# Nine unread products of 16 columns behind the unread product that follows the turning of Q(0)

## The chip, the cores and the metric

The kernel runs on one core of one Trainium2 chip. The metric is the device time in microseconds (us) of one execution. The engines are named as in the profile: PE is the matrix engine TensorE (PEld are its weight loads), DVE is VectorE, ACT is ScalarE, POOL is GpSimd and SP is SyncE, which here only issues DMA transfers. Line numbers (L633) are those of the kernel before the change.

## The reference

What is computed is a recurrence over 768 tokens for 4 x 8 heads of 48 columns, and then a gated feed-forward block over its output, rearranged to 3072 tokens of 384 columns. All of it is in fp32.

```python
# q, k, v: (4, 8, 768, 48), beta: (4, 8, 768)
k_n = k / (np.linalg.norm(k, axis=-1, keepdims=True) + 1e-06)
state = np.zeros((B, H, D, D))
for t in range(S):
    kt, vt, bt = k_n[:, :, t], v[:, :, t], beta[:, :, t, None]
    y[:, :, t] = einsum('bhd,bhde->bhe', q[:, :, t], state)
    v_old = einsum('bhde,bhd->bhe', state, kt)
    state = state + bt[:, :, :, None] * einsum('bhd,bhe->bhde', kt, vt - v_old)
x = y.transpose(0, 2, 1, 3).reshape(3072, 384)
g = x @ w_gate                                   # w_gate, w_val: (384, 1536)
out = (g * (1 / (1 + exp(-g))) * (x @ w_val)) @ w_out    # w_out: (1536, 384)
```

## The kernel before

The 768 tokens are cut into 12 chunks of 64. For each chunk `c` the recurrence is solved in closed form from small products: K times its transpose and Q times the transpose of K (64 x 64 for each head), the inverse of a triangular matrix, and products with the running state. The feed-forward block takes the tokens of a chunk as soon as its output x is there. Its weights are loaded and converted in pieces while the first chunks are prepared.

The whole order of instructions on PE, ACT, DVE, SP and POOL is written by hand: each engine executes its instructions in the order in which the program issues them, under a manual schedule, and semaphores between the engines are the only waits. There is no planner that would move an instruction.

The first part of the program prepares the chunks 0 to 3. The names that matter:

- `turned(c, of_q)` (L484 to L488) transposes K or Q of chunk c on PE, eight transposes of 128 x 128 into two PSUM banks, and ACT copies the two banks to SBUF (`kt`, `qt`). For K(0), K(1) and Q(0) it copies each bank as it is ready (L486), later both at the end (L488).
- `first_gram(c)` (L640) and `gram_steps(c, of_q)` (L498) are the 64x64x64 products of 32 heads, four of which share the PE array at a time. Their results are copied by ACT (L518, L523).
- `low_copies(c)` (L667) are ACT's copies of parts of the first products.
- `first_substitution()` (L700, L706) and `first_z()` (L710) are the triangular inverse on DVE, and `spread_z` (L723, L725) its spreading into `zt`.
- `n_products(c)` (L733) are the next products of 32 heads on PE, which read `zt`; `n_copies` (L739) takes them out.
- `first_advance()` (L952 and following lines), `advance(c)` (L1138 to L1236) and `of_state(c)` (L921) are the steps of the recurrence; `gate_val` (L1562) and the later forms (L1405, L1682) the feed-forward products.
- `stage(n)` (L261, L262) issues on SP the load of one piece of a weight.
- `unread(count, p, m=512)` (L633) issues `count` products on PE whose result nobody reads. Each multiplies a constant 128 x 32 tile `half` with one column of it, repeated m times, and writes 32 rows and m columns of a PSUM bank that is free at that moment:

```python
    def unread(count, p, m=512):
        for _ in range(count):
            nc.tensor.matmul(p[0:R, 0:m], half, half[:, 0:1].to_broadcast([128, m]))
```

The program before the change has unread products in six places: three ahead of the first transposes, one behind the turning of Q(0), four ahead of n_products, and two single ones of 256 columns between the transposes of the first output. The order around the change is this:

```python
        for n in range(6):
            stage(n, n - 2 if n > 1 else None)
        unread(1, banks("p_t", "py")[0])
        turned(2, False, "py")
        first_q = [gram_steps(0, True, 0, (copy_a, copy_a))]
        next(first_q[0])
        gram(2, False, "px", (copy_a, copy_a))
```

The unread product and the transposes of K(2) behind it write the same pair of PSUM banks, `p_py`.

Of the kernel before, what the change touches and what calls it, by code (L numbers as in the profile page):

```python
# [20 lines left out]
def kernel(  # L21
# [51 lines left out]
    def ps_pair(name, tag):  # L73

        return pairs_of_banks[tag]
# [7 lines left out]
    def ps_ffn(shape, name, bank=None):  # L83
        if bank is None:
            taken.append(name)
            bank = (len(taken) - 1) % 4
        n = 1
        for m in shape[1:]:
            n *= m
        p = ffn_banks[bank][:, 0:n]  # L90
        return p if len(shape) == 2 else p.rearrange("p (x n) -> p x n", x=shape[1])
# [16 lines left out]
    def kn_of(c):  # L108
        return knp[c if c < AHEAD else c % 2]

    def kt_of(c):
        return kts[c] if c < AHEAD else kts_late[c % 4]
# [47 lines left out]
    def load_blocks(of_q, c, pars=(0, 1)):  # L160

        x, _, t = blocks_of[of_q]
        x_v = x.rearrange("b (j par) s d -> par s b j d", par=2)
        t_v = t.rearrange("p bp h d -> p (bp h d)")
        t_v = t_v.rearrange("p (b j blk d) -> p b j blk d", b=B, j=NJ, blk=C // R)
        for par in pars:
            for at in range(0, D, R):
                m = min(R, D - at)
                rows = slice(64 * par + at, 64 * par + at + R)
                for blk in range(C // R):  # L170
                    lo = c * C + R * blk
                    nc.sync.dma_start(
                        out=t_v[rows, :, :, blk, 0:m].rearrange("p b j d -> p (b j) d"),
                        in_=x_v[par, lo : lo + R, :, :, at : at + m].rearrange(
                            "s b j d -> s (b j) d"
                        ),
                    )
# [75 lines left out]
    def stage(n, after=None, queue=nc.sync):  # L253
        _, src, t, f0, m = pieces[n]
        name, lo = place_of[n]
        if name not in places:
            places[name] = words(p_places[0])
        place = places[name][:, lo : lo + 2 * m]
        staged[n] = place
        if after is not None:  # L260
            nc.gpsimd.tensor_copy(place[:, 0:1], staged[after][:, 0:1])  # L261
        queue.dma_start(  # L262
            out=place, in_=src[t * 128 : (t + 1) * 128, f0 : f0 + m].bitcast(U32)
        )
# [187 lines left out]
    def banks(name, tag):  # L452

        if type(tag) is int:
            return [ps_ffn([128, 512], name, tag + i) for i in range(2)]
        p = ps_pair(name, tag)
        return [p[:, 0], p[:, 1]]

    def turned(c, of_q, tag=None):

        if tag is None:
            tag = "py" if of_q else "px"
        x = qpad[c % QB] if of_q else kn_of(c)
        if of_q:
            xt = work.tile([128, NB * NJ * 2 * C], FP32, name="qt", bufs=1)
        else:
            xt = kt_of(c)
        if c >= blocks_of[of_q][1]:
            xt_v = xt.rearrange("p (b bp j i) -> p bp j b i", bp=NB, b=2, j=NJ)
            (qt if of_q else kt)[c] = xt_v  # L470
            blocks = blocks_of[of_q][2]
            nc.vector.transpose(xt, blocks.rearrange("p bp h d -> p (bp h d)"))
            spent.append(1.8)
            if c + 1 < NCH:
                for par in range(2):
                    late_loads.append(lambda par=par: load_blocks(of_q, c + 1, (par,)))
            return
        xt = xt.rearrange("p (bp j b i) -> p bp j b i", bp=NB, j=NJ, b=2)
        (qt if of_q else kt)[c] = xt
        p_t = banks("p_t", tag)  # L480
        for bp in range(NB):
            for j in range(NJ):
                at = slice(128 * j, 128 * j + 128)
                nc.tensor.transpose(p_t[bp][:, at], x[:, bp, 2 * j : 2 * j + 2], ident)  # L484
            if type(tag) is int:
                nc.scalar.copy(xt[:, bp].rearrange("p j b i -> p (j b i)"), p_t[bp])  # L486
        for bp in range(NB if type(tag) is not int else 0):
            nc.scalar.copy(xt[:, bp].rearrange("p j b i -> p (j b i)"), p_t[bp])  # L488
# [141 lines left out]
# [4 lines that stand above are left out]
# [1285 lines left out]
    with tc.manual_schedule(  # L1919
# [34 lines left out]
        for n in range(6):  # L1954
            stage(n, n - 2 if n > 1 else None)
        unread(1, banks("p_t", "py")[0])
        turned(2, False, "py")
        first_q = [gram_steps(0, True, 0, (copy_a, copy_a))]
        next(first_q[0])
# [147 lines left out]
```

## Time and profile before

| | |
|---|---|
| median of three runs | 663.82 us (661.48 to 665.75) |
| the profiled execution | 663.32 us |
| span of its instructions | 661.6 us |
| mean granted TensorE clock | 0.995 |
| PE busy | 649.8 us (98%), 10854 records |
| PE weight loads busy | 596.5 us (90%) |
| DVE, ACT, POOL busy | 475.0, 281.3, 198.7 us |
| instruction queue q8 | 85 packets, 1.39 MB |

The span runs from the first to the last instruction of the program; the rest of the execution's time lies around it. A busy share is an average over the span; PE is at 98% because of the long feed-forward part, while its idle time lies mostly in the first 70 us. A product in fp32 appears as two records of PE, each with a weight load (PEld) of its own. "issue" as the reason of an idle time means that the engine waited for nothing that the profile shows.

### The profile page before, as it was taken

What the parts mean: (1) busy time and instruction counts of PE and PEld (TensorE: products, weight loads), DVE (VectorE), ACT (ScalarE), POOL (GpSimd) and SP (SyncE); (2) the same over time, 40 slices, a digit from 0 to 9 for tenths busy, and PEclk for the clock granted to TensorE, in tenths of its full rate; (3) what the DMA queues carried; (4) which work ended last, traced back from release to release, by engine and by line L of the source; (5) the groups of instructions that cost most, each with busy time, mean ns of one, the idle gap of its engine ahead of it and who ended that gap; (6) DMA issues with size and microseconds to landing.
All of it is one profiled execution on the core that took longest, in us unless ns stands there. A gap on an engine that the chain in (4) does not pass through costs nothing.

```text
span 661.6 us, 24916 instructions
## 1 busy us (share of the span) xinstructions
PE 649.8 (98%) x10854; PEld 596.5 (90%) x10854; DVE 475.0 (72%) x989; ACT 281.3 (43%) x626; POOL 198.7 (30%) x312
## 2 busy tenths in 40 slices
PE   8989999999999999999999999999999999999997
PEld 4667888767999999999999999999999999999997
DVE  6779699999689767758667758667758655655563
ACT  4887757224435433434532533532433432333230
POOL 8030041013894032880031881030882000000000
PEclk8989999999999999999999999999999999999999
DMA  9659763005742451364464264364263442232220
GB/s 138 144 165 265 214 145 119 1 14 92 201 78 73 97 122 51 84 142 89 99 127 92 61 152 104 81 131 105 62 142 88 93 109 67 58 97 65 81 72 25
DMA packets 147438, 68.57 MB, mean 104 GB/s; under 512 B 123456, under 2 KB 126560, under 8 KB 147328
## 3 DMA queue, kind: packets, MB, share of 16 engines
q1 hardware_dynamic: 144832, 66.28, 42.8%
q8 instruction: 85, 1.39, 0.9%
q10 hardware_dynamic: 2240, 0.59, 0.5%
q0 software_dynamic: 256, 0.10, 0.2%
q14 instruction: 25, 0.20, 0.1%
HBM read 59.08 MB, written 7.86 MB: 101 GB/s over the span
## 4 chain that ended last, share of the span: by engine, by line
PE 86%; DVE 7%; SPq 3%; issue 2%; DMA 1%; ACT 1%; POOL 0%; DVEq 0%; ACTq 0%; POOLq 0%
PE ffn L1405 39%; PE ffn L1682 21%; PE ffn L1562 9%; PE ffn L1591 2%; SPq L139 2%; PE p_px L1167 2%; PE p_py L498 1%; DVE x_t L583 1%; DVE zb L589 1%; PE p_px L921 1%; PE p_py L1069 1%; PE p_py L1086 1%; PE p_px L1150 1%; PE p_px L498 1%; SPq L185 1%
## 5 line engine op out<-in xcount | busy, mean ns | idle before, releaser
L1405 PE MATMUL ffn<-x_t,w_gv 128*128 128x128 f32 x800 | 108.7, 279 | 0.9 <-DVE p_sb L1632 0.8
L1405 PEld LDWEIGHTS ffn<-x_t,w_gv 128*128 128x128 f32 x800 | 97.4, 192 | 4.1 <-DVE p_sb L1632 2.0
L1439 ACT ACTIVATE sil<-ffn 128x256 f32<-128x256 f32 x100 | 36.4, 383 | 115.3 <-PE ffn L1405 108.0
L1405 PE MATMUL ffn<-x_ffn,w_gv 128*128 128x128 f32 x640 | 84.6, 275 | 0.0
L1682 PE MATMUL ffn<-wo_sb,h_f 128*128 128x192 f32 x480 | 83.9, 328 | 0.0
L1682 PEld LDWEIGHTS ffn<-wo_sb,h_f 128*128 128x128 f32 x480 | 77.9, 190 | 0.6
L1405 PEld LDWEIGHTS ffn<-x_ffn,w_gv 128*128 128x128 f32 x640 | 78.0, 192 | 0.3
L820 POOL TENSOR_TENSOR n_b<-mb,half 128x32 f32<-128x32 f32 x5 | 27.9, 5582 | 161.4 <-DVE mb L552 161.4
L583 POOL TENSOR_TENSOR h_f<-zb,mb 128x31 f32<-128x31 f32 (+15 forms) x124 | 69.4, 559 | 19.2 <-PE p_py L798 6.0
L589 POOL TENSOR_TENSOR zb<-zb,h_f 128x31 f32<-128x31 f32 (+15 forms) x124 | 70.8, 571 | 9.7
L1405 PE MATMUL ffn<-x_t,h_f 128*128 128x128 f32 x472 | 64.7, 280 | 0.0
L1405 PEld LDWEIGHTS ffn<-x_t,h_f 128*128 128x128 f32 x472 | 57.3, 192 | 1.6 <-DVE ffn L1632 0.5
L1440 DVE TENSOR_TENSOR h_f<-sil,ffn 128x256 f32<-128x256 f32 x100 | 39.3, 418 | 24.0 <-ACT sil L1439 24.0
L1101 ACT COPY x_ffn<-p_py 32x256 f32<-32x256 f32 (+3 forms) x108 | 39.4, 365 | 29.0 <-PE p_py L1086 27.3
L1632 DVE TENSOR_TENSOR ffn<-p_sb,ffn 128x512 f32<-128x512 f32 x40 | 27.8, 696 | 25.9 <-PE ffn L1405 25.2
L1635 DVE TENSOR_TENSOR ffn<-ffn,p_sb 128x512 f32<-128x512 f32 x40 | 27.5, 691 | 19.9 <-PE ffn L1405 19.0
L1682 PE MATMUL ffn<-last_k,h_f 128*128 128x192 f32 x200 | 36.0, 327 | 0.0
L1635 DVE TENSOR_TENSOR o_sb<-o_sb,ffn 128x192 f32<-128x192 f32 x50 | 17.5, 350 | 24.2 <-PE ffn L1682 23.5
L1562 PE MATMUL ffn<-x_t,w_gv 128*128 128x256 f32 x144 | 33.9, 385 | 0.2 <-DVE x_t L1041 0.2
L1682 PEld LDWEIGHTS ffn<-last_k,h_f 128*128 128x128 f32 x200 | 32.9, 190 | 0.1
L1562 PE MATMUL ffn<-x_ffn,w_gv 128*128 128x256 f32 x144 | 31.9, 380 | 0.0
L1405 PE MATMUL ffn<-x_ffn,h_f 128*128 128x128 f32 x232 | 30.9, 276 | 0.0
(330 smaller groups left out, 1171.8 us busy)
## 6 DMA issues: line engine op xcount, KB each, us to landing
h_f<-w_s SPq DMA_DIRECT2D x81, 256.0 KB, 2.8
more_w<-w_s SPq DMA_DIRECT2D x27, 256.0 KB, 2.7
vin<-in_v_dram SPq DMA_DIRECT2D x48, 96.0 KB, 3.5
out_dram<-o_sb SPq DMA_DIRECT2D x46, 96.0 KB, 2.2
kn<-in_k_dram SPq DMA_DIRECT2D x20, 192.0 KB, 4.5
zt<-in_moe_w_out_dram SPq DMA_DIRECT2D x10, 384.0 KB, 4.2
qpad<-in_q_dram SPq DMA_DIRECT2D x36, 64.0 KB, 3.0
w_s<-h_f SPq DMA_DIRECT2D x7, 256.0 KB, 2.6
```

The costliest lines, as they stand in the source:

```text
L139: dmas[b % len(dmas)].dma_start(out=t[64 * b : 64 * b + 64, :, :, 0:D].rearrange("p bp h d -> p (bp h) d"), in_=halves(x, c, b).rearrange( ...
L583: engine.tensor_tensor(out=t_v, in0=zb[:, 0 : j + 1, j : j + 1].to_broadcast([128, j + 1, m]), in1=mb[:, j : j + 1, j + 1 : R].to_broadcas ...
L589: engine.tensor_tensor(out=zb[:, 0 : j + 1, j + 1 : R], in0=zb[:, 0 : j + 1, j + 1 : R], in1=t_v, op=ALU.add,)
L820: nc.gpsimd.tensor_tensor(out=n, in0=mb.rearrange("p j i -> p (j i)")[:, 0 : R * R : R + 1], in1=half, op=ALU.pow,)
L1101: nc.scalar.copy(x_all[at % 128 : at % 128 + rows, at // 128].rearrange("p (bp b i) -> p bp b i", bp=NB, b=2), p[64 * half + lo : 64 * hal ...
L1405: nc.tensor.matmul(p[:, u], w(u), moving, start=start and u == 0, stop=True, skip_group_check=True,)
L1439: nc.scalar.activation(silu_of, p[:, 0:2], ACTF.Silu)
L1440: nc.vector.tensor_tensor(out=h_of(c, PAIRS[r][e % 3], e // 3), in0=silu_of, in1=p[:, 2:4], op=ALU.mult)
L1562: nc.tensor.matmul(ps[name][:, i], w_sb[:, t, (f + i) * 128 : (f + i + 1) * 128], xts[c][:, t], start=(t == 0 and i == 0), stop=(t == KT - 1),
L1632: nc.vector.tensor_tensor(out=out, in0=a, in1=b, op=ALU.subtract)
L1635: nc.vector.tensor_tensor(out=out, in0=a, in1=b, op=ALU.add)
L1682: nc.tensor.matmul(p[x, part], a(f - f % 2)[:, f % 2], b(f), start=not begun and f == 0, stop=f == FH - 1, skip_group_check=True,)
```

## The change

Behind the single unread product that follows the turning of Q(0), and ahead of the transposes of K(2), nine more unread products are issued. Each has 16 columns in the place of 512, and writes to the same bank.

```diff
         for n in range(6):
             stage(n, n - 2 if n > 1 else None)
         unread(1, banks("p_t", "py")[0])
+        unread(9, banks("p_t", "py")[0], 16)
         turned(2, False, "py")
         first_q = [gram_steps(0, True, 0, (copy_a, copy_a))]
```

The instructions of ACT, DVE, POOL and SP stay the same and in the same order; on PE, nine products stand between the unread product and the first transpose of K(2), and everything else is as it was.

## The prediction

> **What bounds the kernel now.** I read the page's busy line and slices first, then the waits of PE (TensorE matmul), then PE's timeline around the edit, then stretches cut by the clock.
>
> ```profile
> span 661.6 us, 24916 instructions
> PE 649.8 (98%) x10854; PEld 596.5 (90%) x10854; DVE 475.0 (72%) x989; ACT 281.3 (43%) x626; POOL 198.7 (30%) x312
> ...
> q8 instruction: 85, 1.39, 0.9%
> ```
>
> PE is busy 649.8 of 661.6 us. All that it idles is 11.8 us, so hardly anything can be gained, and whatever delays PE at a place without a wait behind it goes into the end. The edit sits 16.7 us into the span, in the preparation, where PE and ACT hand work to each other:
>
> ```profile
> 15.11 1.67 PE L633 MATMUL p_py<-half 128*32 128x512 f32 x2
> 16.71 1.09 PE L484 MATMUL p_py<-ident,kn 128*128 128x128 f32 x8
> 17.74 1.16 PE L498 MATMUL ffn<-qt,kt 64*64 64x64 f32 x64
> 19.44 1.18 PE L498 MATMUL p_px<-kt 64*64 64x64 f32 x64 [0.55 <-ACT kt L488]
> ...
> 21.86 1.06 PE L484 MATMUL p_px<-ident,qpad 128*128 128x128 f32 x8 [0.21 <-issue]
> 22.86 1.16 PE L498 MATMUL p_py<-last_k 64*64 64x64 f32 x64
> 24.15 1.16 PE L498 MATMUL p_px<-qt,kt 64*64 64x64 f32 x64
> ```
>
> Columns: start, duration, engine, line, tiles, records, and in brackets the idle time before. The nine products go between the first and the second row (no wait stands between: 15.11 + 1.67 runs into 16.71). The first idle time behind them is 0.55 us, ahead of the product of K(2) at 19.44: ACT, in order, was busy with L667 until 18.7 and then copied kt. From there each PE step waits for an ACT copy and each ACT copy for PE, up to the four unread products at 25.24 (end 28.80) and n_products (L733) at 28.80. ACT idles 1.52 us before it can copy that result at 30.06, so there PE is late and not ACT: what PE loses ahead of 28.80 beyond the 0.55 us is lost.
>
> The waits of PE name a second thing, idle time for which no engine is to blame:
>
> ```profile
> PE p_px L952 <- issue: 0.8, 2, 0.5
> PE p_px L1194 <- issue: 0.7, 1, 0.7
> PE ffn L733 <- issue: 0.6, 1, 0.6
> ...
> PE p_px L921 <- issue: 0.2, 1, 0.2
> ```
>
> They strike in the middle of runs of equal products. Adding up the record counts of PE's timeline from the start, they stand behind records 600, 728, 983, 1367 and 1495: distances of 128, 255, 384 and 128, that is multiples of 128 (one record of the trace is missing). A matmul record has a weight load beside it, so 128 records are 256 instructions, and the q8 row gives 2 x 10854 / 85 = 255 instructions a packet. So PE's instructions come in blocks of 256, one packet each, and PE stops at a block's edge when the next one is late. The packets of that queue in the trace confirm it: one starts at 29.47, takes 0.92, and PE goes on at 31.69; 32.80 + 1.02, on at 35.15; 43.50 + 1.07, on at 46.00; 59.89 + 1.51, on at 62.75; 65.35 + 1.06, on at 67.85. A block can be used 1.30 to 1.44 us after it has landed. Its packet starts after PE has entered the block before: 1.0 to 1.1 us later where the loads are quiet (31.69 to 32.80, 46.00 to 47.03), 2.25 us (23.14 to 25.39) and 4.25 us (55.64 to 59.89) where weights are being loaded.
>
> **The change part by part.** (1) *Nine products on PE.* An unread product is two records with two weight loads (the one at 15.11 is x2), so 18 records, 36 instructions. No other engine gets, loses or moves an instruction; no DMA; no wait (same engine, same bank). The trace has no 16-column full-height product. Lower bound: the 64x48 and 64x64 products, four of which share the array, pass at 17 ns a record (64 in 1.08 us): 18 x 17 = 0.31 us. Upper bound: the 128x128 transposes behind them pass at 107 ns with eight times the columns: 1.93 us. Nearest is the weight load of this very product: two were started 28 ns apart (15.106 and 15.134), and with 16 columns the product itself is taken to be no longer. 18 x 28 = 0.5 us, at the full clock, granted again from 16.41. Of this the wait at 19.44 hides 0.55: cost 0 (0 to 1.4; with the cover gone 0.5). The Trainium skill, "TensorE: Matmul & The Clock Gate", section "Wait — 56ns, not 53.3ns?", says that one setting lets the sequencer spend about 62 ns a matmul; an estimate by that is 18 x 62 = 1.1 us, 0.6 of it uncovered. The 17 ns a record speak against that setting here.
>
> (2) *36 instructions ahead of every later block edge.* Every edge falls 18 records earlier in the program. I go through those that matter.
> - Edge A, now at record 344 and later: the edge 472 (n_products, 28.97) moves to 454, the last but one record of Q(1)'s product at 25.08. Its block must come earlier too. The edge before it, which starts the packet, moves from the product at 22.86 into the transposes at 21.86, issued together, so 22.0 instead of 23.14. The loads of v are still running; the row nearest in load is the packet that started 0.8 us behind the edge at 18.25 and took 1.43. With the 1.0 of the quiet rows: start 23.0, landed 24.45, usable at 25.8: PE stops 0.7 us. Bounds: nothing (packet at 22.6 taking 0.94), and 2.6 us (packet at 25.39 as before, usable at 27.7). I take 0.7. Behind it stand the two last records, then the unread products and n_products, so it counts in full.
> - The stop of 0.28 at 31.69 goes: its edge is crossed at 25 instead of 29, the packet has time. -0.28.
> - The stop of 0.54 at 35.15 moves to 710, in the product before: the run from edge to edge is as short as it was. 0 (-0.5 to +0.6).
> - The stop of 0.62 at 46.00 goes: the edge before it falls at 38.0 instead of 40.94, ahead of the weight loads. -0.62.
> - Edge C: the stop of 0.74 at record 1368 moves to 1350, the third of six L1562 records at about 60.6 instead of 62.0. The edge that starts its packet moves only from 55.64 to 55.36, in the stretch where the loads hold the packet back until 59.89 (usable 62.75). The stop becomes about 2.0 us (0.7 to 2.15): +1.26.
> - The 0.19 at 67.85: its edge moves ahead of L921 by 0.6 us and the chain is later: -0.19.
> - Beyond 70 us the edges have at least 0.1 us in hand after the same shift: 0.
>
> Sum: 0 + 0.7 - 0.28 + 0 - 0.62 + 1.26 - 0.19 = +0.87 us. The profiled execution took 663.32 us (span 661.6 and 1.7 around it), so 664.2; the median, 663.82, lies 0.5 above that execution, and by it 664.7. That is 0.13%: about 1% (6.6 us) is what a measurement of this kernel can tell from no change; its three runs alone spread over 4.3 us.
>
> **The rivals.** *Nothing but a hidden delay.* The products fit under the 0.55 us, and the blocks come in time at the new edges because an earlier edge also asks earlier. Time 663.8. For it: the 0.55 us; against: five stops that fit the block edges. The Trainium skill, "Runtime: NRT & Kernel Launch", section "Instruction fetch mechanics", says blocks of 256 instructions are fetched ahead and the cost of an edge is mostly hidden, which would give this time. The trace agrees on the 256, and disagrees on hidden for the five.
>
> *The stops go.* Edges move out of the dense runs and no new stop appears: -(0.28 + 0.54 + 0.62 + 0.74 + 0.19) = -2.4 us, 661.4. For it: three of the five edges get more room; against: 454 and 1350, where the need moves forward more than the request.
>
> *The clock, on the slower side.* The granted clock falls to a half for 3.41 us at a time:
>
> ```profile
> 9.58:13.00 3.42, 3.02 (x82) 2.05 (x80) 2.48 (x6) 2.11 (x5) 3.42 (x2) 1.00 1.29 160
> 13.00:16.41 3.41, 3.41 (x13) 1.75 (x10) 3.05 (x8) 2.10 (x6) 1.73 (x4) 0.50 1.15 147
> ...
> 33.48:36.89 3.41, 2.08 (x113) 1.77 (x109) 3.16 (x7) 2.61 (x8) 1.94 (x4) 1.00 0.38 114
> 36.89:40.31 3.42, 3.21 (x69) 2.16 (x62) 1.76 (x5) 2.34 (x7) 0.49 (x3) 0.50 0.32 115
> ...
> 60.78:64.20 3.42, 2.68 (x71) 2.09 (x70) 2.89 (x7) 2.84 (x8) 0.00 (x0) 1.00 1.01 314
> ```
>
> Stretch, its length, PE busy, then the other engines, the granted clock third from the end. A stretch with 1.33 us of PE idle (33.48) was followed by one at 0.50; one with 0.74 (60.78) was not. So the point from which it decides lies between, and a stop of 2.0 at C, or of over 1 at A, can cross it. Price: half of 3.41, 1.7 us, each. One or two such stretches: 666.4 to 668.1. Three (behind A, behind C, and a second one around 40 since the phase of short waits slides against the grid), with A at 1.5: 664.7 + 0.8 + 5.1 = 670.6, slower by over 1%. Against it: the grid need not fall so that one stop lies in one stretch.
>
> **How the numbers follow.** Forecast 0.38; hidden 0.16; stops gone 0.14; one or two half-clock stretches 0.18; three or more 0.10; 0.04 for a gain of over 1% that I can't name, since 11.8 us of idle are all there is. So slower 0.10, same 0.38 + 0.16 + 0.14 + 0.18 = 0.86, faster 0.04. The range, 661.0 to 669.5, reaches from "stops gone" to two half-clock stretches with A at its upper half, and leaves out the last two cases.
>
> **What would show it.** Right: 18 new L633 records in about 0.5 us and the wait ahead of 19.44 nearly gone with its start unmoved; "issue" stops 18 records earlier in the program, one near 25.1 at the end of Q(1)'s product, one in L1562 near 60.6, none at n_products of chunk 1 (46.0). Wrong: the stops at their old instructions, which would refute the blocks; L633 records at 100 ns each; or a change of over 6 us, for which the clock rows would have to show new stretches at 0.50.

## The result, and the profile after

The changed kernel takes 664.94 us (median of 22 runs, 662.26 to 667.31), the kernel before 662.53 us (median of 22 runs on the same chips). The ratio is 1.0031, with a 95% interval of 1.0016 to 1.0046: 2.05 us slower, between 1.1 and 3.0 us. Forecast were +0.87 us, 664.7 us, and no difference that a measurement of this kernel could tell; it is a loss of 0.3%, and it takes this many runs to show it.

The page of the kernel after, the lines that answer to those shown of before:

```profile
span 665.1 us, 24952 instructions
PE 650.2 (98%) x10872; PEld 597.5 (90%) x10872; DVE 475.9 (72%) x989; ACT 280.9 (42%) x626; POOL 198.4 (30%) x312
...
q8 instruction: 85, 1.39, 0.8%
```

There are 18 records more and 36 instructions more, as forecast, and PE's busy time grows by 0.4 us. The span of this one execution is 3.5 us longer than that of the one before. Single executions of one kernel differ by more than that: the 22 of the kernel before reach from 660.5 to 668.6 us. The timeline of PE after (start, duration, line, tiles, records, idle time before):

```profile
14.28 1.60 PE L633 MATMUL p_py<-half 128*32 128x512 f32 x20
15.82 1.09 PE L484 MATMUL p_py<-ident,kn 128*128 128x128 f32 x8
16.84 1.16 PE L498 MATMUL ffn<-qt,kt 64*64 64x64 f32 x64
18.66 1.18 PE L498 MATMUL p_px<-kt 64*64 64x64 f32 x64 [0.66 <-ACT kt L488]
...
24.72 0.21 PE L498 MATMUL p_px<-qt,kt 64*64 64x64 f32 x1 [0.20 <-issue]
...
31.09 0.37 PE L952 MATMUL p_py<-vin,zt 64*64 64x48 f32 x10 [0.71 <-issue]
...
39.54 0.66 PE L952 MATMUL p_py<-uu,p_sb 64*64 64x48 f32 x10 [0.82 <-issue]
...
58.65 1.01 PE L1194 MATMUL p_px<-v,zb 64*64 64x48 f32 x51 [1.24 <-issue]
```

The first row holds the old unread product and the nine new ones; in the single records the new ones start 31.6 ns apart, 18 x 31.6 = 0.57 us, where 0.5 was forecast. They end under a wait for ACT (0.66 us at 18.66), so they cost nothing there. Then come the "issue" stops. Counted from the start they stand behind records 473, 600, 728 (34.55 us, 0.38), 856, 983 (47.50, 0.10) and 1239: the same grid of 128 as before, and so other instructions of the program, 18 records earlier. Each of these is a block edge; which edges stop PE has changed.

Of the largest waits of PE after, the third is one that before did not have:

```profile
PE p_py L952 <- issue: 1.9, 3, 0.8
PE p_px L1194 <- issue: 1.2, 1, 1.2
PE ffn L1405 <- DVE zt L907: 1.2, 1, 1.2
```

It is a single stop of 1.24 us, 540 us into the span, half a millisecond behind the edit. It stands behind the last of the joins (L903, 128 short records in 1.2 us). PE's timeline there, first of before and then of after:

```profile
534.36 1.29 PE L903 MATMUL p_py<-t,z 32*32 32x32 f32 x128
535.58 1.16 PE L1405 MATMUL ffn<-x_t,w_gv 128*128 128x128 f32 x8
536.57 1.06 PE L1405 MATMUL ffn<-x_ffn,more_w 128*128 128x128 f32 x8
...
538.36 1.06 PE L1405 MATMUL ffn<-x_ffn,h_f 128*128 128x128 f32 x8
```

```profile
536.34 1.29 PE L903 MATMUL p_py<-t,z 32*32 32x32 f32 x128
537.56 1.16 PE L1405 MATMUL ffn<-x_t,w_gv 128*128 128x128 f32 x8
539.96 1.13 PE L1405 MATMUL ffn<-x_ffn,more_w 128*128 128x128 f32 x8 [1.24 <-DVE zt L907]
...
541.82 1.06 PE L1405 MATMUL ffn<-x_ffn,h_f 128*128 128x128 f32 x8
```

From the start of the join to the last of these rows PE takes 4.00 us before and 5.48 us after: the stop costs 1.48 us of time, more than its length, since rows that follow each other without a stop overlap.

The name behind the arrow is a copy on DVE that ends just then, at 539.93. The same product of before started at 536.57, while that copy was still to come (536.73 to 537.95), so it doesn't need it. What the trace of after has instead is a packet of the instruction queue that starts at 537.48, with the end of the join, lands at 538.36, and 1.6 us later PE goes on.

A smaller stop stands behind an earlier join of 128 records, at record 4169, again at a block edge:

```profile
246.60 0.49 PE L1405 MATMUL ffn<-x_t,h_f 128*128 128x128 f32 x3 [0.84 <-issue]
```

Before has no stop there. From the start of that join (241.94 after, 239.97 before) to the L1069 product behind it (248.81, 246.31) PE takes 0.53 us more than before. In the other four traces with 18 records added (e1, e3, e4 and e8 below) the stop is 0.29, none, 0.36 and 0.38 us, and PE takes only 0.00 to 0.08 us more, since a wait for DVE of 0.20 us close behind it falls away. So it adds to the loss of this one execution, and little to that of the others.

**The theory** that the experiments test: PE's instructions come in blocks of 256; a block is asked for when PE enters the one before it, and can be used some 3.5 us later (in the eight traces that stop behind this join 3.3 to 4.0: 0.9 to 1.3 until its packet starts, 0.9 to 1.7 of transfer, 1.3 to 1.7 until it is used). A stop comes where a block of short records is used up in less. Such a stop is a wait of its own beside the semaphores, which the description of the kernel before called the only waits. The 36 added instructions move every edge behind them, and at 537 us a block now holds 120 of the join's short records and 8 wide ones. **The rivals**: the PE time of the nine products; their place; a wait for data of fixed length behind the join.

### The profile page after: what moved, and what is told of

The parts are those of the page before. It is cut to its first block, busy times and chain, and to the rows that moved or that the text cites. A ratio compares the mean times of both kernels' runs of the same rounds, so it can differ in the third digit from the quotient of the medians.

```text
span 665.1 us, 24952 instructions
## 1 busy us (share of the span) xinstructions
PE 650.2 (98%) x10872; PEld 597.5 (90%) x10872; DVE 475.9 (72%) x989; ACT 280.9 (42%) x626; POOL 198.4 (30%) x312
## 4 chain that ended last, share of the span: by engine, by line
PE 90%; DVE 6%; ACT 2%; issue 1%; DVEq 0%; ACTq 0%
PE ffn L1405 39%; PE ffn L1682 21%; PE ffn L1562 9%; PE ffn L1591 2%; PE p_px L1167 2%; PE p_px L498 2%; PE p_py L498 1%; DVE x_t L583 1%; DVE zb L589 1%; PE p_py L1069 1%; PE p_px L921 1%; PE p_py L1086 1%; PE p_px L1150 1%; PE ffn L633 1%; PE p_px L633 1%
## 5 line engine op out<-in xcount | busy, mean ns | idle before, releaser
L1405 PE MATMUL ffn<-x_t,w_gv 128*128 128x128 f32 x800 | 108.6, 279 | 0.7 <-DVE p_sb L1632 0.5
L1405 PEld LDWEIGHTS ffn<-x_t,w_gv 128*128 128x128 f32 x800 | 97.4, 192 | 3.5 <-DVE p_sb L1632 1.4
L1405 PE MATMUL ffn<-x_ffn,w_gv 128*128 128x128 f32 x640 | 84.6, 276 | 0.0
L1405 PEld LDWEIGHTS ffn<-x_ffn,w_gv 128*128 128x128 f32 x640 | 78.0, 192 | 0.3
L1405 PE MATMUL ffn<-x_t,h_f 128*128 128x128 f32 x472 | 64.9, 280 | 0.8 <-issue 0.8
L1405 PEld LDWEIGHTS ffn<-x_t,h_f 128*128 128x128 f32 x472 | 57.4, 192 | 2.5 <-issue 0.9
L1405 PE MATMUL ffn<-x_ffn,h_f 128*128 128x128 f32 x232 | 31.0, 277 | 0.0
```

The source lines that it names most:

```text
L1405: nc.tensor.matmul(p[:, u], w(u), moving, start=start and u == 0, stop=True, skip_group_check=True,)
```

## The experiments

Times are ratios to the kernel before with 95% intervals, over runs on the same chip; they are 0.2 to 0.3% wide on each side, as large as the effect, so the traces carry most of the proof.

**e1_wide10: the edges without the time.**

```diff
-        unread(1, banks("p_t", "py")[0])
+        unread(10, banks("p_t", "py")[0], 51)
```

> The unread product of 512 columns and the nine of 16 become ten of 51 columns: 20 records as with the change, so every block edge lies where the change has it, but with about the PE time of the kernel before (20 records of about 43 ns, 0.86 us, as the one product took). Theory of the block edges: the time of the change, about 2 us above before (+0.3%), with issue stops at records 473, 600, 728, 856 counted from the start and none at 1368. Theory of the added PE time: no difference to before, under 0.3 us.

Measured: ratio 1.0014 (0.9993 to 1.0034), which fits either theory. In its trace the stops stand behind records 473 (0.55 us), 600 (0.25), 728 (1.48) and 1239 (0.41), none at 856 or 1368 (that of 856 was forecast, that of 1239 was not), and at 539.02 us, behind the join, there is the stop of the changed kernel, 1.22 us. So the stop follows the number of instructions, not the added PE time.

**e2_time_only: the time without the edges.**

```diff
         unread(1, banks("p_t", "py")[0])
+        unread(1, banks("p_t", "py")[0], 352)
```

> One more unread product of 352 columns in the place of the nine: about 0.6 us of PE as the nine took, but 2 records in the place of 18, so the block edges move by 2 records only. Theory of the block edges: within 0.5 us of before, stops at the instructions of before (two records earlier), the wait ahead of the product of K(2) shorter by 0.55 to 0.6 us. Theory of the added PE time: as the change, about 2 us above before.

Measured: ratio 1.0004 (0.9984 to 1.0025). The stops stand at records 600, 728, 983 and 1239, and behind the join one of 0.13 us is left. PE time alone does not bring the late stop. The wait ahead of the product of K(2) was 0.62 us here; it did not shrink against the 0.55 of the first trace of before, because ahead of it the clock's half-speed stretch (13.0 to 16.4 us there) didn't fall in this execution. Executions without that stretch and without added products have 1.06 to 1.22 us there (e3, e4, e5, e7 and e9), so the half microsecond is hidden, as forecast.

**e3_mid18: the edges moved at another place.**

```diff
-        unread(4, banks("p_t", 2)[0])
+        unread(13, banks("p_t", 2)[0], 160)
```

> Nothing is added behind the turning of Q(0); the four unread products of 512 columns ahead of n_products become thirteen of 160: 26 records in the place of 8, about the same 3.6 us, so the edges from there on lie 18 records earlier as with the change, and those ahead of it where the kernel before has them. Theory of the block edges: as the change without its small stop at the end of Q(1)'s product, +1.5 to +2.3 us, with stops in the products of vin, uu and p_sb (records 600, 728, 856). Theory that the place behind the turning of Q(0) matters: no difference to before.

Measured: ratio 1.0008 (0.9989 to 1.0027), +0.5 us, below the forecast of +1.5 to +2.3 us, into which the interval reaches (-0.7 to +1.8 us). Early stops: 0.18 at 600, 0.93 at 728, none at 856, 1.03 at 1239. The late stop is there again, 1.23 us at 538.32, though nothing was added at the turning of Q(0): the place is no cause.

**e4_late9: the nine products 150 us later.**

```diff
         finish(2)
+        unread(9, banks("p_t", "py")[0], 16)
         first_x_sums(2)
```

> The nine products are issued ahead of the first x sums of chunk 2, behind the first two outputs, and not at the turning of Q(0). PE is dense there, so their 0.6 us count in full; the edges of the first 150 us stay. Theory of the block edges: stops of the first 70 us as before, +0.6 us (0 to 1.2). Theory that nine products cost 2 us wherever they stand: +2 us.

Measured: ratio 1.0024 (1.0005 to 1.0043), +1.6 us, more than the block theory's point of 0.6 that left out the late stop. All edges of the first 150 us are those of before; the products stand at 168.8 us, and the stop behind the join is 1.23 us. From the start of the join to the L1405 row of h_f it takes 5.46 us, 1.46 more than before; with the 0.57 of PE time that makes 2.0 us, inside the interval (0.3 to 2.9). So this run loses about as much as the change with nothing altered in the preparation, but the 0.57 us, which the change hides, are part of it.

**e5_late13 and e6_late4: the dose.** The same place, thirteen products and four.

```diff
         finish(2)
+        unread(13, banks("p_t", "py")[0], 16)     # e6: unread(4, ...)
         first_x_sums(2)
```

> Thirteen products at the late place (ahead of the first x sums of chunk 2) in the place of nine: the edges behind it move by 26 records. The block that ends behind the join of the last chunks (L903, about 537 us) then holds the 128 short join records alone, so its successor, asked for at the join's first record, needs about 3.3 us and the block is used up in 1.3. Theory of the block edges: a stop of about 2.0 us at the first L1405 products behind that join (1.23 with nine), time +2.8 us (0.8 of PE and 2.0). Theory of a data wait of fixed length at that place: 1.2 us as with nine. Theory that only PE time counts: +0.8 us.

> Four products at the late place: edges 8 records earlier, ten wide records more of the block are left between the join and the edge than with nine. Theory of the block edges: the stop behind the join at 537 us falls to 0 to 0.3 us, time +0.25 to +0.6 us. Theory of a wait of fixed length: 1.2 us as with nine, +1.5 us.

Measured: ratios 1.0095 (1.0062 to 1.0128) and 1.0001 (0.9978 to 1.0025). The join in PE's timeline, thirteen products first and four second:

```profile
541.03 1.29 PE L903 MATMUL p_py<-t,z 32*32 32x32 f32 x128
544.49 2.07 PE L1405 MATMUL ffn<-x_t,w_gv 128*128 128x128 f32 x8 [2.17 <-issue]
546.36 1.57 PE L1405 MATMUL ffn<-x_ffn,more_w 128*128 128x128 f32 x8
```

```profile
534.00 1.29 PE L903 MATMUL p_py<-t,z 32*32 32x32 f32 x128
535.22 1.16 PE L1405 MATMUL ffn<-x_t,w_gv 128*128 128x128 f32 x8
536.21 1.06 PE L1405 MATMUL ffn<-x_ffn,more_w 128*128 128x128 f32 x8
537.11 0.28 PE L1405 MATMUL ffn<-x_ffn,w_gv 128*128 128x128 f32 x1
537.91 0.94 PE L1405 MATMUL ffn<-x_ffn,w_gv 128*128 128x128 f32 x7 [0.53 <-issue]
```

The stop has moved with the edge: directly behind the join with thirteen, 8 records later with nine, 17 later with four. Its length is 2.17, 1.23 and 0.53 us (forecast 2.0 for the first and 0 to 0.3 for the last). A wait for data would stay at one product; this one does not, and in these two traces it is named "issue". From the start of the join to the L1405 row of h_f PE takes 4.00 us where the edges are those of before or a few records later (before, e10, e7, e9), 4.31 with 2 records added (e2), 4.68 with 8 (e6), 5.45 to 5.48 with 18 (after, e1, e3 and e4; 5.20 in e8) and 7.63 with 26 (e5). That settles the late stop.

With thirteen the loss, 6.3 us, is more than the 2.8 us forecast. Stretches of that run (length, busy times, granted clock third from the end) show one reason:

```profile
540.60:544.01 3.41, 1.72 (x133) 1.49 (x131) 1.46 (x3) 1.45 (x3) 0.00 (x0) 1.00 0.73 146
544.02:547.43 3.41, 2.94 (x14) 2.94 (x15) 0.60 (x1) 0.57 (x1) 0.00 (x0) 0.50 0.04 9
```

PE was busy for 1.72 of 3.41 us, and the next 3.41 us went at half the clock: eight products took 2.07 us in the place of 1.16. That is the rival of the clock, with its price of up to 1.7 us; behind the stops of 1.23 us at this place the clock stayed whole. Stop and slow stretch are 3.6 us (7.63 less 4.00), the thirteen products 0.8, and a stop at another late edge (446.33 us) 0.45. That leaves 1.4 of the 6.3 us. The profiled execution also lost time in its first 70 us (a stop of 2.46 us at record 1239 and two half-speed stretches behind it), with edges that are those of before; how much of it other executions of the kernel share is open.

**e7_period128: a whole block more.**

```diff
-        unread(4, banks("p_t", 2)[0])
+        unread(68, banks("p_t", 2)[0], 16)
```

> The four unread products of 512 columns ahead of n_products become 68 of 16: 136 records in the place of 8, 256 instructions more, one whole block. Every edge behind it lies at the record of the program where it lay before, one block later in number. The unread products take 68 x 2 x 32 ns = 4.3 us in the place of 3.6. Theory of the block edges: no stop behind the join at 537 us and the early stops at the products where before has them; +0.7 us. Theory that the number of added instructions counts: seven times the change's late stop and time, +5 us or more.

Measured: ratio 1.0055 (1.0036 to 1.0073), +3.6 us: neither the 0.7 nor the 5. The trace bears out the places. Behind the join there is no stop, and the early ones stand at 728, 856, 1111 and 1367, which are 600, 728, 983 and 1239 of before, one block on. So seven times as many instructions bring no late stop at all, when the edges come back to where they were. What the forecast left out is the edge at 472, which now lies in the middle of the unread products:

```profile
25.99 3.91 PE L633 MATMUL ffn<-half 128*32 128x16 f32 x119 [1.23 <-issue]
```

That is 0.7 + 1.23 = 1.9 us; the remaining 1.7 fits early stops that were longer in this execution (1.20, 0.81, 0.89 and 2.12 us), but one trace can't show that they always are.

**e8_after_again and e10_before_again: the same kernels, a second trace.**

> The changed kernel once more, for a second trace. Theory of the block edges: the stop of 1.2 us behind the join at 537 us again to within 0.1 us, the stops of the first 70 us at the same records but of other lengths, since there the packets wait among the loads of the weights; no stop at record 1368 or 1496.

> The kernel before once more, for a second trace. Theory of the block edges: issue stops again at records 600, 728, 983, 1239, 1367 or 1495 and at no others of the first 70 us, of other lengths than in the first trace, no stop of over 0.6 us behind the join at 537 us; the 70th us is reached within 1 us of the first trace, counted in instructions.

Measured (after): spans 662.8 us now, 665.1 first. Early stops 1.17 at 473, 0.24 at 600, 1.20 at 728, and none at 856 or 1239, none of more than 0.05 us at 1368 or 1496. The late one:

```profile
537.70 1.13 PE L1405 MATMUL ffn<-x_ffn,more_w 128*128 128x128 f32 x8 [0.97 <-DMA qpad<-in_q_dram]
```

It is at the same product and shorter by 0.27 us (0.1 was expected). Here the copy on DVE ended at 537.94, 0.24 us after PE had gone on, so DVE was not what PE waited for; the arrow names yet another bystander.

Measured (before): span 661.3 us. Early stops 1.22 at 600, 0.82 at 728, 1.17 at 983 and 0.44 at 1239, none behind the join; record 1495 starts 0.28 us later than in the first trace. These are places that were expected, but 1367 and 1495, which stopped in the first trace, did not stop. Off the grid stands only the 0.22 us ahead of the transposes of Q(1) (record 320) that is named "issue" in the first trace too; the expectation had left it out.

**e9_trim2: a version that might have been faster.**

```diff
-        unread(4, banks("p_t", 2)[0])
+        unread(2, banks("p_t", 2)[0])
```

> The kernel before with two unread products of 512 columns ahead of n_products in the place of four: 1.8 us less of PE there, 4 records fewer, so the edges behind lie 4 records later. The trace of before has zt ready at 27.33 and n_products at 28.80, held by the unread products. Theory of PE order: n_products start at about 27.4, 1.4 us earlier, the stop behind the join at 537 us stays away, time -1.0 to -1.4 us. Rival (the clock): the idle time ahead of n_products halves the clock for 3.41 us, time 0 to +1.5 us. Rival (the block edge at n_products): the packet of that block lands at 26.3 to 26.5 and holds PE until 27.7, time -0.8 us.

Measured: ratio 1.0002 (0.9984 to 1.0021). n_products started at 27.07 us, 1.73 us earlier than in the first trace of before, but only 0.75 earlier than in e4 (27.82), which has the program of before up to there and, like this run, no half-speed stretch ahead of it. A wait of 0.41 us stands before them:

```profile
24.76 1.91 PE L633 MATMUL ffn<-half 128*32 128x512 f32 x4
27.07 1.16 PE L733 MATMUL ffn<-zt,a_sb 64*64 64x64 f32 x64 [0.41 <-ACT zt L723]
```

There was no stop behind the join, but against the first trace of before the gain is gone by 43 us, with stops of 0.77 and 1.29 us; two more, of 0.73 and 1.45, follow, and the two half-speed stretches lie together (35.6 to 42.4 us). No version was found that beats the kernel before.

## Why the prediction was right in its range, and which steps failed

The range (661.0 to 669.5) holds the time, the mechanism (block edges moved by 36 instructions) is the one at work, and the sign is right. The size is not well met: the +0.87 us forecast lie just below the interval of 1.1 to 3.0. That 664.7 us came so near to the measured 664.94 is luck: it was counted from 663.82, the median of three runs, which is 1.3 us above the 662.53 of 22 runs. And the sum was made of the wrong terms.

*The nine products*: 0.57 us in the place of 0.5, hidden. Right. The estimate by the 62 ns a matmul of the Trainium skill ("TensorE: Matmul & The Clock Gate", section "Wait — 56ns, not 53.3ns?") does not hold here: a record took 31.6 ns.

*"Beyond 70 us the edges have at least 0.1 us in hand after the same shift: 0."* This step failed; the stop measured about 1.2 us, and 1.2 to 1.5 us of time (1.24, 1.22, 1.23, 1.23 and 0.97 in the five traces with 18 records added, 0.13 or nothing in those of before, e2, e7, e9 and e10). Its reason can be read in the trace: blocks hold instructions, and I had counted matmul records alone. PE's own semaphore instructions fill blocks too, and there are some 120 of them up to 537 us. (The distance of 255 between 728 and 983 was put down to a missing record; two such instructions lie between.) Counted in, the stops of after stand at instructions 960, 1216, 1472, 1729, 1984, 2497, 8384 and 18882: the remainder by 256 is 192 to 194 each time. Without them the late edges were looked for up to 52 records from where they are. At the right place the working would have been short: the block is asked for when the join starts, in both kernels; in it 18 wide records give way to 18 short ones, 18 x (0.11 - 0.01) = 1.8 us less to use, against 0.2 to 0.6 us in hand: in before PE reached this edge 1.9 us after the packet had landed (536.55 and 538.47), where 1.3 to 1.7 are enough.

*Edge C, +1.26 us, the largest term.* It did not come: none of the four traces with early edges moved (after, e1, e3, e8) stops at record 1368 for more than 0.05 us. Instead the edge before it, 1239, stopped PE (1.24, 0.41, 1.03 and 0 us), and by then the loads had let the next packet through (61.18 to 62.12 in after, where PE passed the edge at 63.8). I had kept that packet at the start it had in one trace. The same goes for the stop itself: of the five traces with the edges of before, two stop at 1367 (0.74 and, in e6, 0.30 us) and four at 1239.

*Edge A, 0.7 us*: the stop at the end of Q(1)'s product came, with 0.20, 0.55 and 1.17 us in after, e1 and e8. Right in place, and in the mean of three.

*The savings.* The stop of 0.28 did not go; it moved to record 600 (0.71 in after, 0.25 in e1, 0.18 in e3, 0.24 in e8). That of 0.54 came in each of the four, as forecast, but with 0.38 to 1.48 us. That of 0.62 went in e1, e3 and e8, and in after came as 0.82 at 856 and 0.10 at 983; e4 and e5, with the edges of before, do not have it either. The 0.19 at 67.85 went in all four, and also in e10, e4 and e5.

All stops at block edges from 20 to 70 us together are 3.45, 2.69, 2.14 and 2.61 us in the four traces with early edges moved (after, e1, e3, e8), and 2.37, 3.65, 1.72, 3.28 and 4.75 in the five with the edges of before (before, e10, e4, e6, e5). No difference can be seen between them. The time at which PE comes to record 1495 of before is 69.8, 69.5, 68.9 and 68.3 us in the four, and 67.9, 68.1, 68.6, 67.8 and 73.8 in the five, which hints at a loss of up to 1 us but is too few traces to tell. So the early terms of my sum, taken from one trace to a hundredth of a microsecond, are within what one execution differs from the next. The late stop, 1.2 to 1.5 us of time, is the part of the 2.05 us that is shown; it alone lies within the interval of 1.1 to 3.0, and it fits the times of e1 and e3, which have it too (+0.9 us, -0.5 to 2.3, and +0.5 us, -0.7 to 1.8). Whether the early edges, and the stop at 246 us, add the rest stays open. The total came near by an error that was too much (C) and one that was too little (the join).

*The rivals.* "The stops go" and "hidden" fall with the interval above 1. The clock did not decide here: after has 6.8 us at half clock in the first 70 us, as before has, only at other times. But it can: each of the three stops of over 2 us (2.46 and 2.17 in e5, 2.12 in e7) was followed by a half-speed stretch. The point from which the clock falls was put between 0.74 and 1.33 us of idle time in a stretch; the prediction's own first row speaks against that, since 9.58:13.00 has 0.40 us of idle time (3.42 less 3.02) and a stretch at 0.50 behind it. What decides is open.

## What to carry to other kernels

On an engine that is busy 98% of the time, an instruction costs not only its own time but also where it puts the edges of all later instruction blocks; look for runs of over a hundred short instructions, and see what the block that ends behind them holds. Count every instruction of the engine, semaphores included, when you look for an edge. And take the spread between two traces of the same kernel before you add up terms of a few tenths of a microsecond from one.

## What the runs showed of the hardware that was not expected

An edit 16 us into a program had its clearest effect 520 us later, with no data and no semaphore between them, only PE's own stream of instructions. The reason that a trace gives for such a stop can be any neighbour: the stop behind the join was put down to a DVE copy (after), a DMA (e8) and "issue" (e5). The Trainium skill, "Runtime: NRT & Kernel Launch", section "Instruction fetch mechanics", has the block of 256 instructions that these traces confirm, and calls the cost of an edge mostly hidden: of some 85 edges in each trace four to eight stopped PE, for 0.1 to 2.5 us each.

What sets the start of a packet in the first 70 us is open. It came 0.35 to 5.8 us after PE had entered the block before, the long times often while the loads of the weights ran. That is not all of it: in after one started at 28.71, 4.0 us after PE had entered its block, although no load ran from 26.6 to 27.4 us.
